# The p7 of the last two first channel products as seven smaller products, with another order of the pair's blocks

## The chip, the cores and the metric

The kernel runs on one core of a Trainium2 chip. The metric is the device time of one execution in microseconds (us); lower is better. Before the change the median of three runs is 796.17 us (796.07, 796.17 and 796.9).

## The reference

The program computes an attention block with a mask from hashes, and an MLP mixer over its output. All inputs are float32. Cut to what is computed:

```python
# q, k, v: (4, 8, 768, 64)
mask = q_bucket[..., :, None] == k_bucket[..., None, :]   # 6 sign bits of q @ proj, k @ proj
scores = np.where(mask, q @ k.T / 8, -1e9)
attn = softmax(scores) @ v            # (B, S, H*D) = x: (4, 768, 512)
h = np.maximum(x.T @ w_tok1, 0) @ w_tok2      # over the 768 tokens
u = x + h.T
h2 = np.maximum(u @ w_ch1, 0) @ w_ch2         # 512 -> 1536 -> 512 channels
out = u + h2
```

The change concerns the first channel product, `u @ w_ch1`, with its ReLU.

## The kernel before, in words

There are three stages, one after the other: attention (one pair of heads at a time), the token mixing, and the channel mixing (`channels`). The 3072 rows of u lie transposed in the on-chip tile `XT` (512 channels in four blocks of 128, by 3072 rows).

`channels` takes the rows in three steps, s = 0, 1, 2, of 1024 rows each (two halves of TT = 512). A step first makes the hidden values (the first channel product with ReLU), then the outputs (`outputs(s)`, the second channel product).

Both products use the Strassen-Winograd scheme: a product of 2 x 2 blocks is made of seven block products p1 to p7 instead of eight, and of sums of the blocks. The left operand is a weight, the right one activations. Sums of weight blocks are in `SW1` and `SW2`, sums of activations in `T[0]` to `T[3]` (buffers `TA` and `TB`). Results go to `R[0]` to `R[3]`.

At s = 0 the hidden values come from `hidden(0, t)` for six t, with whole block products. Between them, jobs of `prepare` make the sums that a second level of the same scheme needs of the weights, and store them, with the raw quarters, to DRAM: `second_parts` for the second channel product, `hidden_parts` for four products of the first (p2, p6, p3, p4). A job makes four sums on the Vector engine (DVE), in one of two scratch places, and issues its stores on SP's queue. One place is the tile `seen`, the other a part of the tile `second1`. The list of jobs has twelve entries, and `hidden` takes one of them in its middle and one after it (call at line 817 and on; jobs at 1057 to 1060, stores at 1068 to 1078).

At s = 1 and 2 the hidden values come from `hidden_pair(s, t, between)` for t = 0, 1, 2 (GP = 3), which makes two of the six blocks at a time. In it p1, p5 and p7 are whole products (`whole`: two groups of matmuls of 512 columns), and p2, p6, p3 and p4 are objects of the class `Smaller`, each of seven matmuls of 256 columns, one second-level product each:

- `one` makes the first quarter product, and the Activation engine (ACT) copies it out of the bank (line 897).
- `three` makes three products that can be added at once to quarters of a bank pair that holds something else already (the "direct quarters").
- `rest` makes the other three; the last of them is added to the bank that ACT copied in `one`. It then issues on SP's queue the fetch of the left parts that stand five objects later (`fetch_hidden_left`, line 860). Left parts of 448 KB lie in five places in turn (`hidden_left_at`).
- `finish` copies a quarter out on ACT (line 918) and makes two sums on DVE (lines 920 and 923).

The right parts of a smaller product are the four quarters of its right block and four sums of them; `right_sums` makes these on DVE (lines 846 to 849) once for each s: p2's in `outputs(s - 1)`, p6's ahead of the first pair, p3's and p4's inside the first pair (`between`).

Four PSUM bank pairs (b0 to b3, two banks of 512 columns each) are given out by hand in `ring`. The engines run in the order that the code is written in (`manual_schedule`), with waits by semaphores where one engine needs another. `plus` (line 955) is an add on DVE, `copy` (952) and `relu` (958) are on ACT. `end_rows` runs the end of the pair before: three ReLUs and the difference r[1] - r[0].

`look()` is another matter: it checks the sizes of q and k, four times a pair. It squares a tile fetched earlier on ACT (lines 1297 and 1298) and has the GpSimd queue (POOL) fetch the next (line 1308). POOL also issues the stores that add to the output (line 1223).

In `outputs(s)`, `product` makes a second-level product of 21 matmul groups, about 9.06 us each, with its right sums made on DVE just ahead (`begin`, lines 1131 and 1132; `combine`, line 1136; lines 1171 and 1174), and `fetch_left` (line 1114) fetches the left parts two products ahead.

All matmuls of `channels` are issued at line 780, in `accumulate`.

Of the kernel before, what the change touches and what calls it, by code (L numbers as in the profile page):

```python
# [36 lines left out]
F32 = mybir.dt.float32  # L37
# [11 lines left out]
def kernel(  # L49
# [13 lines left out]
    nc = tc.nc  # L63
    P = 128
# [9 lines left out]
    NHT = DCH // P  # L74
    HALF = S // 2
    GR = NR // 2
    TT = 512
# [674 lines left out]
    def channels(pool, psum, SW1, second, TA, judge):  # L752
# [7 lines left out]
        last = B * S // (2 * TT) - 1  # L760
# [7 lines left out]
        def bank_pair(i):  # L768
            return psum.tile([P, 2, TT], F32, name=f"b{i}", tag=f"b{i}", bufs=1)
# [66 lines left out]
        def right_sums(name, s):  # L836


            sl = [slice(TT * (2 * s + i), TT * (2 * s + i) + TT) for i in range(2)]
            src = {"p2": XT[:, KC:, sl[0]], "p3": XT[:, KC:, sl[1]], "p6": T[1], "p4": T[3]}[name]  # L840
            z = split4(XT[:, SMALLER.index(name), : 2 * TT])
            half = [slice(0, TT // 2), slice(TT // 2, TT)]
            b = [src[:, k, n] for k in range(2) for n in half]

            def job():
                nc.vector.tensor_tensor(z[:, 0], b[1], b[0], op=ALU.subtract)
                nc.vector.tensor_tensor(z[:, 1], b[3], b[1], op=ALU.subtract)
                nc.vector.tensor_tensor(z[:, 2], b[3], z[:, 0], op=ALU.subtract)
                nc.vector.tensor_tensor(z[:, 3], b[2], z[:, 2], op=ALU.subtract)

            return job, [*b, *(z[:, i] for i in range(4))]

        def split4(a):
            return a.rearrange("p (n t) -> p n t", n=4)

        def fetch_hidden_left(h):

            if h < 4 * GP * last:
                t = h // 4 % GP
                nc.sync.dma_start(  # L860
                    out=hidden_left_at(h).rearrange("p (i c) -> p i c", i=7),
                    in_=hidden_passed[SMALLER[h % 4]][:, :7, P * t : P * t + P],
                )

        def hidden_left_at(h):
# [10 lines left out]
        def first_weight(name):  # L876

            return {
                "p2": WC1[:, KC:, : DCH // 2], "p3": SW1[:, 2], "p4": WC1[:, KC:, DCH // 2 :], "p6": SW1[:, 0],
            }[name]  # L880

        def kept(name):
# [3 lines left out]
        class Smaller:  # L886
# [12 lines left out]
            def three(self, pair, start=False):  # L899

                self.mm(pair[:, 0, : TT // 2], 5, 2, start)
                self.mm(pair[:, 0, TT // 2 :], 3, 3, start)
                self.mm(pair[:, 1, : TT // 2], 6, 7, start)

            def rest(self):
# [19 lines left out]
        def hidden_pair(s, t, between):  # L925


            sl = [slice(TT * (2 * s + i), TT * (2 * s + i) + TT) for i in range(2)]
            ks = range(KC)
            r = [a[:, :, t::GP].rearrange("p n i c -> p i n c") for a in R]  # L930
            x, z, e, y = ring
            ring[:] = [y, e, x, z]

            p1, e2 = [output_at(i).rearrange("p i n -> p (i n)") for i in (0, 2)]
            p5, e6, u = copies(), copies(), copies()
            e3, e4 = p1, e2
            h = 4 * GP * (s - 1) + 4 * t
            p2, p6, p3, p4 = [Smaller(h + i, name, s) for i, name in enumerate(SMALLER)]

            def rows(a):  # L940
                return a.rearrange("p (i n c) -> p i n c", i=2, n=2)

            def banks(a):
                return a.rearrange("p i (n c) -> p i n c", n=2)

            def whole(pair, left, right, which=(0, 1)):
                for i in which:
                    at = P * (t + GP * i)
                    accumulate(pair[:, i], lambda k: left(k)[:, at : at + P], right, ks)

            def copy(to, pair):
                nc.scalar.copy(to.rearrange("p (i n) -> p i n", i=2), pair)

            def plus(to, a, b):
                nc.vector.tensor_tensor(to, a, b, op=ALU.add)

            def relu(i):
                nc.scalar.activation(r[i], r[i], ACT.Relu)

            X = bank_pair(x)  # L960
            whole(X, lambda k: WC1[:, k], lambda k: XT[:, k, sl[0]])
            Z, E = bank_pair(z), bank_pair(e)
            copy(p1, X)
            p2.one(E, e2)
            p2.three(Z, True)
            Y = bank_pair(y)
            whole(Y, lambda k: WC1[:, k, DCH // 2 :], lambda k: T[0][:, k], [0])
            n = TT * 3 // 2
            plus(p1[:, :n], Z.rearrange("p i n -> p (i n)")[:, :n], p1[:, :n])
            end_rows()  # L970
            p2.rest()
            whole(Y, lambda k: WC1[:, k, DCH // 2 :], lambda k: T[0][:, k], [1])
            p2.finish()
            copy(p5, Y)
            look()
            plus(r[0], rows(p1), rows(e2))
            for job in between:
                job()
            E = bank_pair(z)
            p6.one(E, e6)  # L980
            p6.three(X)
            copy(u, X)
            V = bank_pair(e)
            whole(V, lambda k: SW1[:, 1, k], lambda k: T[2][:, k])
            p6.rest()
            look()
            plus(rows(p5), banks(V), rows(p5))
            p6.finish()
            relu(0)
            plus(u, u, e6)  # L990
            E3 = bank_pair(x)
            p3.one(E3, e3)
            look()
            p3.three(Y)
            p4.three(V)
            p4.one(bank_pair(z), e4)
            plus(r[1], banks(Y), rows(u))
            plus(r[2], banks(V), rows(u))
            plus(r[3], rows(p5), rows(u))
            p3.rest()  # L1000
            p4.rest()
            p3.finish()
            plus(r[1], r[1], rows(e3))
            p4.finish()
            plus(r[2], r[2], rows(e4))
            look()

            def end():
                relu(3)
                relu(1)  # L1010
                relu(2)
                nc.vector.tensor_tensor(r[1], r[1], r[0], op=ALU.subtract)

            unfinished.append(end)

        SMALLER = ["p2", "p6", "p3", "p4"]
        GP = HC // 2
        hidden_passed = second["hidden_passed"]  # L1020


# [8 lines left out]
        def prepare():  # L1031
# [42 lines left out]
            def hidden_parts(name):  # L1074
                def store(place, raw, rest):
                    nc.sync.dma_start(out=hidden_passed[name][:, :4], in_=place)
                    for there, here in zip(kept(name), [*raw, rest]):
                        nc.sync.dma_start(out=there, in_=here[:, 0])

                return parts(first_weight(name), store, SMALLER.index(name) % 2 == 0)  # L1080

            sums = weight_sums(WC2, SW2, slice(0, HC), slice(HC, NHT), low, high)
            return [
                [], sums, [whole("p1"), second_parts("p7")], *([second_parts(name)] for name in ("p6", "p3", "p5", "p2", "p4")),
                *([hidden_parts(name)] for name in SMALLER),
            ]

        def area(i):
# [257 lines left out]
        for s in range(1, last + 1):  # L1346
            right_sums("p6", s)[0]()
            for t in range(GP):
                hidden_pair(s, t, [right_sums(name, s)[0] for name in ("p3", "p4")] if t == 0 else [])
                if t == 0:  # L1350
                    residual(s)
            outputs(s)
# [7 lines left out]
    def with_token_weights(stage):  # L1360
        with tc.tile_pool(name="tok", bufs=1, reuse_waits="tile") as tok:
# [7 lines left out]
    n = NHT // 4 * P  # L1369
    second = {  # L1370
        "hidden_passed": {
            f"p{i}": dram.tile([P, 8, NHT // 4 * P], F32, name=f"hidden_left{i}") for i in (2, 3, 4, 6)
        },
        "passed": {
            f"p{i}": dram.tile([P, (4 if i == 1 else 7) * n], F32, name=f"left{i}") for i in range(1, 8)
# [99 lines left out]
```

## Time and profile before

One profiled execution took 795.47 us; its span, from the first instruction of the program to the last, is 793.7 us. The rest of the time is start and end.

| what | value |
|---|---|
| median of the runs | 796.17 us |
| profiled execution | 795.47 us |
| its span | 793.7 us |
| TensorE matmul (PE) busy | 787.1 us, 99% |
| Vector engine (DVE) busy | 660.0 us, 83% |
| Activation engine (ACT) busy | 441.6 us, 56% |
| GpSimd (POOL) busy | 53.5 us, 7% |
| bytes moved by DMA | 138.67 MB, mean 175 GB/s |
| matmul records of 512 columns, line 780, TA and SW (p7, in all three steps) | 72, 592 ns each |
| matmul records of 256 columns, line 780, XT and SW | 96, 379 ns each |

How to read it: a float32 matmul leaves two records, each with its weight load (PEld, 190 ns). The records overlap, so a record's length isn't the time that it takes from the engine; that is the distance from one start to the next. A group line names the line of the code, the engine, the operation, and what it writes and reads (`b<-TA,SW`: into a bank from the tiles TA and SW). A timeline line has the start from the beginning of the span, the length, the engine, line, operation and tiles, how many were merged, and, in brackets, how long the engine was idle before it and who ended that.

Where the stages lie in the span: attention to about 310 us, token mixing to 387.6, `hidden(0, t)` to about 459.6, `outputs(0)` to about 524.3, the three pairs of s = 1 to 591.4, `outputs(1)` to about 656, the three pairs of s = 2 and `outputs(2)` to the end.

### The profile page before, as it was taken

The page shows a single profiled execution, that of the slowest core. Times are in us where ns is not written, and L with a number is a line of the kernel's source. Part 1 is how long each engine was busy: PE and PEld are TensorE (multiplying, and loading weights), DVE is VectorE, ACT ScalarE, POOL GpSimd, SP SyncE. Part 2 cuts the span into 40 slices and gives each one's busy share as a digit, 9 for nine tenths or more (in the row PEclk, how much of TensorE's full clock was granted, in tenths as well). Part 3 has the DMA queues.
Part 4 walks back from the last instruction along what each step waited for, and adds up shares of the span by engine and source line. Part 5 has one row for each costly group of instructions (what it writes and reads, how often), then busy time and mean ns, then how long its engine had stood idle before and what let it go on. Part 6 is the DMA issues. An engine that isn't in the chain of part 4 may idle for free.

```text
span 793.7 us, 12166 instructions
## 1 busy us (share of the span) xinstructions
PE 787.1 (99%) x4661; PEld 464.9 (59%) x4661; DVE 660.0 (83%) x885; ACT 441.6 (56%) x706; POOL 53.5 (7%) x77
## 2 busy tenths in 40 slices
PE   9999999999999999999999999999999999999997
PEld 5444444444444444455544458876667886666886
DVE  5989898988987677999688698988769897778986
ACT  6688888888888886333223221337773335775111
POOL 1000000000000000011121010111110012000001
PEclk9999999999999999999999999999999999999999
DMA  4435353537452415796726993699754578630456
GB/s 164 163 123 163 123 163 123 163 126 239 151 179 85 153 43 168 220 275 175 176 62 228 339 350 140 188 299 294 200 151 143 215 204 195 213 109 1 152 173 158
DMA packets 90974, 138.67 MB, mean 175 GB/s; under 512 B 29656, under 2 KB 63392, under 8 KB 88608
## 3 DMA queue, kind: packets, MB, share of 16 engines
q1 hardware_dynamic: 82752, 112.86, 42.9%
q0 software_dynamic: 7728, 24.64, 14.1%
q8 instruction: 38, 0.62, 0.3%
q10 hardware_dynamic: 432, 0.34, 0.2%
q14 instruction: 24, 0.20, 0.1%
HBM read 97.21 MB, written 33.16 MB: 164 GB/s over the span
## 4 chain that ended last, share of the span: by engine, by line
PE 99%; DVE 0%; issue 0%; DVEq 0%
PE b L780 50%; PE sc L353 20%; PE acc L407 16%; PE t L653 5%; PE t L693 5%; PE sums L431 2%; PE hp L301 1%; PE idle L470 0%; PE hw L325 0%; DVE second L1203 0%; DVE ones L97 0%; PE b L1320 0%; DVEq L1470 0%
## 5 line engine op out<-in xcount | busy, mean ns | idle before, releaser
L360 ACT ACTIVATE e<-sc 128x768 f32<-128x768 f32 x192 | 154.2, 812 | 11.1 <-PE sc L353 10.8
L353 PE MATMUL sc<-qk 64*128 64x384 f32 x768 | 153.1, 484 | 0.0
L780 PE MATMUL b<-R,second 128*128 128x256 f32 (+1 forms) x612 | 150.9, 404 | 0.0
L780 PEld LDWEIGHTS b<-R,second 128*128 128x128 f32 x612 | 116.3, 190 | 31.6 <-issue 17.2
L786 ACT COPY c<-b 128x512 f32<-128x512 f32 (+1 forms) x78 | 37.5, 488 | 169.1 <-PE b L780 159.6
L407 PE MATMUL acc<-e,vn 128*32 128x384 f32 x1536 | 127.0, 486 | 0.0
L392 DVE TENSOR_TENSOR esd<-esd,e 128x768 f32<-128x768 f32 x96 | 92.0, 958 | 10.4 <-ACT e L360 0.5
L407 PEld LDWEIGHTS acc<-e,vn 128*32 128x32 f32 x1536 | 49.9, 110 | 73.9 <-issue 73.3
L353 PEld LDWEIGHTS sc<-qk 64*128 64x128 f32 x768 | 68.4, 188 | 41.8 <-issue 36.7
L780 PE MATMUL b<-XT,WC 128*128 128x256 f32 (+1 forms) x264 | 82.5, 456 | 0.0
L780 PEld LDWEIGHTS b<-XT,WC 128*128 128x128 f32 x264 | 50.2, 190 | 29.6 <-issue 25.1
L353 PE MATMUL sc<-bits 64*128 64x384 bf16 x384 | 62.5, 323 | 0.0
L388 DVE SCALAR_TENSOR_TENSOR esd<-e 128x768 f32<-128x768 f32 x32 | 30.6, 955 | 23.4 <-ACT e L360 23.4
L653 PE MATMUL t<-x,W 128*128 128x512 f32 x96 | 41.8, 593 | 0.0
L353 PEld LDWEIGHTS <-bits 64*128 64x128 bf16 x384 | 18.5, 94 | 33.2 <-issue 8.8
L713 POOL DMA_DIRECT2D XT<-second x8 | 9.9, 1232 | 385.5 <-DVE second L712 368.8
L452 ACT COPY rec<-rec 32x384 f32<-32x384 f32 x64 | 32.6, 510 | 5.0 <-DVE rec L446 4.2
L413 ACT ACTIVATE num<-acc,vsum 128x384 f32<-128x384 f32 x32 | 18.6, 582 | 29.7 <-PE acc L407 29.3
L780 PE MATMUL b<-XT,SW 128*128 128x256 f32 (+1 forms) x120 | 34.6, 422 | 0.0
L780 PE MATMUL b<-TA,WC 128*128 128x512 f32 x72 | 33.8, 592 | 0.0
L780 PE MATMUL b<-TA,SW 128*128 128x512 f32 x72 | 32.9, 592 | 0.0
L395 DVE TENSOR_TENSOR esd<-esd,e 128x768 f32<-128x768 f32 x32 | 30.5, 954 | 1.9
(217 smaller groups left out, 1130.0 us busy)
## 6 DMA issues: line engine op xcount, KB each, us to landing
second<-left SPq DMA_DIRECT2D x18, 1344.0 KB
raw<-in_moe_w_ch SPq DMA_DIRECT2D x16, 768.0 KB
qk<-in_qk SPq DMA_DIRECT2D x15, 768.0 KB
seen<-in_qk POOLq DMA_DIRECT2D x21, 384.0 KB, 4.0
WC<-hidden_left SPq DMA_DIRECT2D x15, 448.0 KB
vn<-in_v SPq DMA_DIRECT2D x16, 384.0 KB
vt<-in_vT SPq DMA_DIRECT2D x16, 384.0 KB
x<-bounced SPq DMA_DIRECT2D x4, 1536.0 KB
```

Of the source, the lines that this page charges most:

```text
L353: nc.tensor.matmul(sc[:, i, :HALF], t[rows, 1, P * c : P * c + P], t[rows, 0, qs], start=start, stop=not start,)
L360: nc.scalar.activation(e, sc[:, :, :HALF], ACT.Exp, scale=SCALE)
L388: nc.vector.scalar_tensor_tensor(self.d, es[0], NR * EPS, es[1], op0=ALU.add, op1=ALU.add,)
L392: nc.vector.tensor_tensor(self.d, self.d, e, op=ALU.add)
L395: nc.vector.tensor_tensor(self.d, self.d, self.es[-1], op=ALU.add)
L407: nc.tensor.matmul(acc[D * i + d : D * i + d + 32], vn[:, i, c, d : d + 32], e[:, i], start=(c == 0), stop=(c == NR - 1),)
L413: nc.scalar.activation(nums[self.n][:, self.half], acc, ACT.Identity, scale=-1.0, bias=vsum,)
L452: nc.scalar.copy(rec[other : other + 32, h], rec[at : at + 32, h])
L653: nc.tensor.matmul(ps, W1[:, r, P * j : P * j + P], x[:, r], start=(r == 0), stop=(r == NR - 1),)
L693: nc.tensor.matmul(ps[at], left, right, start=start, stop=True, skip_group_check=True,)
L780: nc.tensor.matmul(ps, left(k), right(k), start=start and k == ks[0], stop=stop and k == ks[-1], skip_group_check=True,)
L786: nc.scalar.copy(c, ps)
```

## The change

p7 becomes a fifth `Smaller`. What it brings:

- In each of the six pairs, p7's two groups of whole matmuls (four matmuls of 512 columns) become seven matmuls of 256. p7 gets its first quarter `e7` (in the tile `q1`), its `rest` and its `finish`, and one more add, of `e7` to `u`. Its direct quarters fill three quarters of the bank pair V; the fourth stays unused, so the add to p5 takes 768 columns, and r[2] is made in two adds and a copy on ACT.
- p7's right sums are one more job of four DVE operations in the first pair of each s; they lie in `SW1[:, 1]`.
- `hidden_parts("p7")` is one more job at s = 0: four sums and five stores. It shares an entry of the list with p6's, and p7 takes the scratch place in `second1`; p3 moves from that place to `seen`.
- The left parts have five fetches a pair; the object five later is now the same product of the next pair.
- The order inside the pair: p6's direct quarters stand ahead of its first quarter. Behind each first quarter stand the direct quarters of the next product, and then the rest. Behind p4's first quarter stands the first block of the next pair's p1 (`opened`, kept in `ahead`), in the pairs that have a next one. `ring` hands the bank pairs on in another order.
- `Smaller.three` starts the second half of a bank with `start=False`.

```diff
@@ right_sums
-            z = split4(XT[:, SMALLER.index(name), : 2 * TT])
+            if name == "p7":
+                z = SW1[:, 1].rearrange("p k c -> p (k c)")[:, : 2 * TT]
+            else:
+                z = XT[:, ["p2", "p6", "p3", "p4"].index(name), : 2 * TT]
+            z = split4(z)
@@ fetch_hidden_left
-            if h < 4 * GP * last:
-                t = h // 4 % GP
+            if h < 5 * GP * last:
+                t = h // 5 % GP
...
-                    in_=hidden_passed[SMALLER[h % 4]][:, :7, P * t : P * t + P],
+                    in_=hidden_passed[SMALLER[h % 5]][:, :7, P * t : P * t + P],
@@ Smaller.three
-                self.mm(pair[:, 0, TT // 2 :], 3, 3, start)
+                self.mm(pair[:, 0, TT // 2 :], 3, 3, False)
@@ hidden_pair
-            ring[:] = [y, e, x, z]
+            ring[:] = [y, e, z, x]
...
+            e7 = q1.rearrange("p i n -> p (i n)")
-            h = 4 * GP * (s - 1) + 4 * t
-            p2, p6, p3, p4 = [Smaller(h + i, name, s) for i, name in enumerate(SMALLER)]
+            h = 5 * GP * (s - 1) + 5 * t
+            p2, p6, p7, p3, p4 = [Smaller(h + i, name, s) for i, name in enumerate(SMALLER)]
...
-            X = bank_pair(x)
-            whole(X, lambda k: WC1[:, k], lambda k: XT[:, k, sl[0]])
+            def opened(pair, which, s=s, t=t):
+                start = TT * 2 * s
+                whole(pair, lambda k: WC1[:, k], lambda k: XT[:, k, start : start + TT], which, t)
+
+            X = ahead.pop() if ahead else None
+            if not X:
+                X = bank_pair(x)
+                opened(X, [0])
+            opened(X, [1])
...
             copy(p5, Y)
+            plus(r[0], rows(p1), rows(e2))
+            p6.three(X)
+            p6.one(bank_pair(z), e6)
+            copy(u, X)
             look()
-            plus(r[0], rows(p1), rows(e2))
-            for job in between:
+            V = bank_pair(e)
+            for job in between[:2]:
                 job()
-            E = bank_pair(z)
-            p6.one(E, e6)
-            p6.three(X)
-            copy(u, X)
-            V = bank_pair(e)
-            whole(V, lambda k: SW1[:, 1, k], lambda k: T[2][:, k])
+            p7.three(V, True)
             p6.rest()
-            look()
-            plus(rows(p5), banks(V), rows(p5))
+            plus(p5[:, :n], V.rearrange("p i n -> p (i n)")[:, :n], p5[:, :n])
+            for job in between[2:]:
+                job()
             p6.finish()
-            relu(0)
             plus(u, u, e6)
-            E3 = bank_pair(x)
-            p3.one(E3, e3)
+            p7.one(bank_pair(x), e7)
             look()
             p3.three(Y)
+            p7.rest()
+            p7.finish()
+            p3.one(bank_pair(z), e3)
+            relu(0)
             p4.three(V)
-            p4.one(bank_pair(z), e4)
+            p3.rest()
             plus(r[1], banks(Y), rows(u))
-            plus(r[2], banks(V), rows(u))
+            plus(u, u, e7)
+            plus(r[2][:, 0], banks(V)[:, 0], rows(u)[:, 0])
+            plus(r[2][:, 1, 0], banks(V)[:, 1, 0], rows(u)[:, 1, 0])
+            p3.finish()
+            p4.one(bank_pair(x), e4)
+            look()
+            nc.scalar.copy(r[2][:, 1, 1], rows(u)[:, 1, 1])
+            if t + 1 < GP:
+                ahead.append(bank_pair(y))
+                opened(ahead[0], [0], t=t + 1)
+            p4.rest()
             plus(r[3], rows(p5), rows(u))
-            p3.rest()
-            p4.rest()
-            p3.finish()
+            p4.finish()
             plus(r[1], r[1], rows(e3))
-            p4.finish()
             plus(r[2], r[2], rows(e4))
             look()
@@ channels, prepare
-        SMALLER = ["p2", "p6", "p3", "p4"]
+        SMALLER = ["p2", "p6", "p7", "p3", "p4"]
...
-                return parts(first_weight(name), store, SMALLER.index(name) % 2 == 0)
+                return parts(first_weight(name), store, name in ("p2", "p7"))
...
-                *([hidden_parts(name)] for name in SMALLER),
+                [hidden_parts("p2")], [hidden_parts("p6"), hidden_parts("p7")], [hidden_parts("p3")], [hidden_parts("p4")],
@@ the loop over s and t
-                hidden_pair(s, t, [right_sums(name, s)[0] for name in ("p3", "p4")] if t == 0 else [])
+                hidden_pair(s, t, [right_sums(name, s)[0] for name in ("p7", "p3", "p4")] if t == 0 else [])
```

More of the change, by code (lines that the diff above doesn't have):

```diff
@@ L839, in right_sums @@
             sl = [slice(TT * (2 * s + i), TT * (2 * s + i) + TT) for i in range(2)]
-            src = {"p2": XT[:, KC:, sl[0]], "p3": XT[:, KC:, sl[1]], "p6": T[1], "p4": T[3]}[name]
-            z = split4(XT[:, SMALLER.index(name), : 2 * TT])
+            src = {"p2": XT[:, KC:, sl[0]], "p3": XT[:, KC:, sl[1]], "p6": T[1], "p7": T[2], "p4": T[3]}[name]
+            if name == "p7":
[3 more added lines that the diff above has]
+            z = split4(z)
             half = [slice(0, TT // 2), slice(TT // 2, TT)]
@@ L879, in first_weight @@
                 "p2": WC1[:, KC:, : DCH // 2], "p3": SW1[:, 2], "p4": WC1[:, KC:, DCH // 2 :], "p6": SW1[:, 0],
+                "p7": SW1[:, 1],
             }[name]
@@ L944, in banks, with whole @@
                 return a.rearrange("p i (n c) -> p i n c", n=2)
-            def whole(pair, left, right, which=(0, 1)):
+            def whole(pair, left, right, which=(0, 1), t=t):
                 for i in which:
@@ L1014, in hidden_pair @@
             unfinished.append(end)
-        SMALLER = ["p2", "p6", "p3", "p4"]
+        SMALLER = ["p2", "p6", "p7", "p3", "p4"]
         GP = HC // 2
+        ahead = []
         hidden_passed = second["hidden_passed"]
@@ L1371 @@
         "hidden_passed": {
-            f"p{i}": dram.tile([P, 8, NHT // 4 * P], F32, name=f"hidden_left{i}") for i in (2, 3, 4, 6)
+            f"p{i}": dram.tile([P, 8, NHT // 4 * P], F32, name=f"hidden_left{i}") for i in (2, 3, 4, 6, 7)
         },
```

## The prediction

> **What bounds the kernel now.** I read the page's head and chain first, then the chain in order of time, the windows of single stages, and the timelines of the first pair and of SP's queue.
>
> ```profile
> span 793.7 us, 12166 instructions
> ...
> PE 787.1 (99%) x4661; PEld 464.9 (59%) x4661; DVE 660.0 (83%) x885; ACT 441.6 (56%) x706; POOL 53.5 (7%) x77
> ...
> PE 99%; DVE 0%; issue 0%; DVEq 0%
> ```
>
> TensorE is the chain. In order of time (start, length, what) the channel stage is one piece:
>
> ```profile
> 387.63 364.23 PE b L780 x1308
> ...
> 751.97 36.28 PE b L780 x168
> ```
>
> Start-to-start times of the matmuls there are 0.429 us per record of 512 columns and 0.216 per record of 256 (one float32 matmul is two records), with no larger gap. So PE time taken out is worth its full length, and any new wait of PE costs its full length. The windows are the three pairs of s=1, then the stretch in which the parts for later are stored:
>
> ```profile
> 524.27:546.64 22.37, 22.37 (x81) 15.19 (x80) 17.94 (x29) 11.49 (x20) 4.74 (x6) 1.00 1.01 276
> 546.64:569.00 22.36, 22.36 (x81) 15.20 (x80) 16.04 (x19) 16.47 (x27) 2.16 (x4) 1.00 0.81 253
> 569.00:591.40 22.40, 22.40 (x81) 15.21 (x81) 16.08 (x19) 16.47 (x27) 2.15 (x4) 1.00 0.54 151
> ...
> 455.00:470.00 15.00, 15.00 (x37) 6.63 (x36) 13.35 (x21) 3.58 (x7) 3.00 (x4) 1.00 0.96 363
> ```
>
> Columns: length; busy PE, weight load, DVE, ACT, POOL; clock; DMA share; GB/s. A pair takes 22.4 us of PE. DVE has 4.4 us to spare in the first, some 6.3 in the others, ACT 5.9. In 455 to 470 the DMA engines are full.
>
> **What the Trainium skill says.** "TensorE: Matmul & The Clock Gate", section "Wait — 56ns, not 53.3ns?": a warm matmul takes N / 2.4 GHz plus about 2.5 ns. The trace agrees: 1024/2.4 + 2.5 = 429.2 ns, 512/2.4 + 2.5 = 215.8. Smaller blocks cost almost nothing extra. "PSUM — Partial Sum Buffer", section "Engine vs sequencer instructions": ACT and DVE run strictly in order, and matmuls start in order, so what waits holds all behind it; the trace shows no overtaking. "DMA: Bandwidth & Descriptors", section "Queues, rings and completion order": each DMA engine takes a ring's descriptors in order, so an added store delays the loads issued after it on SP. In the trace the load issued at 470.06 follows the stores of 465.05.
>
> **The change, part by part.**
>
> *PE work.* Removed per pair: 4 matmuls of 512 columns, 8 x 0.429 = 3.43 us (535.87 to 539.30 in the first pair). Added: 7 of 256 columns, 14 x 0.216 = 3.02. Gain 0.41 a pair, 2.47 us for six pairs. The next pair's block and the direct quarters only move.
>
> *DVE and ACT per pair.* DVE: + p7's finish (0.69 + 0.42), + adding e7 to u (1.22), - 0.27 for the add to p5 (0.96 for 1.23), - 0.12 for r[2] in two pieces: + 1.9 us, 18 of 22. ACT: three 256-column copies, + 1.1. Both fit; hidden under PE except in the first pair of each s, where DVE also has p7's four sums.
>
> *First pair, layout on the trace's clock.* These rows of before are the anchor:
>
> ```profile
> 531.13 1.46 PE L780 MATMUL b<-XT,WC 128*128 128x256 f32 x6
> 532.63 0.37 ACT L918 COPY second<-b 128x256 f32<-128x256 f32 x1 [3.06 <-PE b L780]
> 533.03 0.69 DVE L920 TENSOR_TENSOR second<-b,second 128x512 f32<-128x512 f32 x1 [2.39 <-ACT second L918]
> 534.14 1.46 PE L780 MATMUL b<-TB,WC 128*128 128x256 f32 x6
> 534.22 1.22 DVE L955 TENSOR_TENSOR R<-second 128x1024 f32<-128x1024 f32 x1
> 536.48 0.42 DVE L849 TENSOR_TENSOR XT<-XT 128x256 f32<-128x256 f32 x1
> 537.95 0.42 DVE L849 TENSOR_TENSOR XT<-TB,XT 128x256 f32<-128x256 f32 x1
> ```
>
> Until 534.14 nothing changes. Then p6 takes four matmuls (1.73) and p7's direct quarters begin at 535.87. Their third needs the last of p7's sums. DVE makes them where it made p3's, so they end at 536.90 (536.48 + 0.42). PE would be there at 536.73. The hand-over to PE: DVE's first memset ends at 1.03 and the weight load waiting for it starts at 1.08, so 0.05; how much of a 0.19 us weight load then lies bare isn't shown for 128 columns, so 0.05 to 0.24; I take 0.14. Stall 0.31. DVE goes on: p3's sums to 538.37, the p5 add to 539.25, p4's sums to 540.7, p6's finish to 541.86. p3's first quarter reuses p6's bank: PE is there at 537.04 + 0.43 + 1.29 + 0.43 + 1.29 + 1.29 = 541.77 and gets it at 542.0: stall 0.23. DVE then has u, p7's finish, r[1], e7, r[2], p3's finish, r[3], p4's finish and the two last adds, 11.6 us, to about 553.5; only then may ACT overwrite e2 (0.04 + 0.37), which p2's rest in the next pair waits for: 554.05, against PE at 542.0 + 11.6 = 553.6 less some 0.2 that DVE's overlapped starts win. Stall 0.2 (0 to 0.6). After that DVE has slack.
>
> *Last pair.* With no next pair, p4's rest stands directly behind p4's first quarter, whose bank ACT must have copied. Matmul start to its end 0.216 + 0.379, to ACT 0.04 (532.59 to 532.63), copy 0.37, hand-over 0.14: 1.15 us, less 0.43 in which the matmul itself runs: stall 0.72 (0.63 to 0.82). In before, p3's rest (1.29) stands there. In the other pairs the opened block, 1.72, covers it; without that cover each would pay 0.72 too.
>
> Sum per s: 0.31 + 0.23 + 0.2 + 0.72 = 1.46, twice 2.9 (2.2 to 4.0).
>
> *Storing p7's parts at s=0.* Four DVE sums (2.2) fall in DVE's gap of 3.76 us before 456.40; the first waits for the store of p2's, whose buffer it takes, about 454.5, so they end at 456.7: DVE 0.3 late, nothing lost. Five stores, 1536 KB = 1.57 MB, at 363 GB/s: 4.3 us more in a full queue.
>
> ```profile
> 452.67 0.32 SPq L1076 DMA_DIRECT2D hidden_left<-seen  x1
> 453.03 3.69 SPq L1078 DMA_DIRECT2D hidden_left<-SW  x4
> 459.70 0.32 SPq L1076 DMA_DIRECT2D hidden_left<-second  x1
> ...
> 464.69 0.32 SPq L1076 DMA_DIRECT2D hidden_left<-seen  x1
> 465.05 2.86 SPq L1078 DMA_DIRECT2D hidden_left<-WC  x4
> 470.06 0.32 SPq L1114 DMA_DIRECT2D second<-left  x1
> ```
>
> p3 now uses `seen`, and p4 right after it, so p4's sums on DVE wait until p3's store has landed: about 462.6 + 4.3 less overlap = 466.4 instead of 462.45, and all DVE work of `outputs(0)` stands 4 us back behind it. These show what it has in hand:
>
> ```profile
> 462.45 0.55 DVE L1057 TENSOR_TENSOR seen<-WC 128x384 f32<-128x384 f32 x1
> ...
> 471.36 0.96 DVE L1171 TENSOR_TENSOR R<-R 128x768 f32<-128x768 f32 x1 [1.37 <-PE b L780]
> 472.66 0.96 DVE L1174 TENSOR_TENSOR R<-R 128x768 f32<-128x768 f32 x1 [0.34 <-PE b L780]
> ```
>
> L1171 would end at 474.9 and PE wants it at 475.05: just in time. 2.3 us of delay are left for the next `begin` (b01 ready at 481.9, wanted by 481.36: 0 to 0.5). p4's stores go out at 468.7 instead of 464.69, so the load of the second product's left parts (L1114, in before landed at 478.2 by its semaphore's last update, wanted at 478.9) lands at 478.7 to 480.7. Both waits overlap. I take 0.5, bounds 0 and 2.2.
>
> *Fetches of left parts in the pairs*: one more per pair (448 KB), each with a pair's length, some 19 us, from issue to use; in before they land 4 to 7 us after issue. Nothing. POOL's order of looks and stores is kept; nothing.
>
> **Sum.** Profiled execution 795.47 (span 793.7): - 2.47 + 2.9 + 0.5 = + 0.9, so 796.4. The three runs' median, 796.17, lies 0.7 above it: 797.1. Bounds: - 2.47 + 2.2 + 0 = - 0.3 (795.9) and - 2.47 + 4.0 + 2.2 = + 3.7 (799.9). About 0.2%, 1.6 us, is what a measurement of this kernel can tell from no change. So: within it, slightly slower.
>
> **Rivals.**
> - *The store backlog decides (slower).* In the stage change at 460 to 480, DVE or PE waits for SP's queue. For it: DMA share 0.96, the load's 0.7 us in hand, the new back-to-back use of `seen`. Against: DVE's idle 1.7 us and the pauses in the queue. From 1.2 us of stall there the whole is slower; at 2.2 it is 796.17 - 2.47 + 2.9 + 2.2 = 798.8.
> - *ACT or DVE falls behind in every pair (slower).* ACT would do 17.6 of 22 us with looks between the critical copies; one us per pair of late copies gives 797.1 + 6 = 803. Against: between first quarter and rest stand 1.29 us, for a round trip of 1.15.
> - *The waits vanish (faster).* If DVE starts the first pair earlier and hand-over is 0.05, only the last pair's 0.63 remains: 796.17 - 2.47 + 1.3 = 795.0; with less still 794.3.
>
> **How the numbers follow.** Forecast case (795.6 to 797.8) 0.54; backlog 0.25, of which nearly all is slower; late copies 0.11; vanished waits 0.10, most of it faster by over 0.2%. That is faster 0.08, same 0.55, slower 0.37. The range 795.4 to 800.4 takes in the forecast's bounds and the backlog, and leaves out the late copies and half of the last.
>
> **What would show it.** PE busy down by about 2.5 us while the span grows; 14 records more per pair of 256 columns and 8 fewer of 512; gaps on PE before the third direct quarter of p7 in the first pair of each s (0.3), before p3's first quarter (0.2), and before p4's rest in the last (0.7); one DVE wait of some 4 us at `seen` near 462. Wrong: a gap over 1 us before the second product's first matmul near 479, gaps in the middle pairs, or none in the last.

## The result and the profile after

The changed kernel takes 797.86 us (median of 15 runs, 797.23 to 798.45), the kernel before 796.17 (15 runs, 794.3 to 797.73). The ratio is 1.0021, with a 95% interval of 1.0013 to 1.0029: 1.7 us slower. The sign is that of the forecast (797.1); the size lies 0.8 us beyond its number, at the edge of the 0.2% that I had called no difference.

The head of the page, and TensorE's share of the chain that ended last:

```profile
span 796.7 us, 12316 instructions
...
PE 786.7 (99%) x4697; PEld 471.0 (59%) x4697; DVE 675.4 (85%) x921; ACT 448.0 (56%) x724; POOL 53.8 (7%) x77
...
PE 92%; DVE 4%; DMA 3%; issue 0%; ACT 0%; DVEq 0%
```

The span grew by 3.0 us, and PE is no longer the whole chain: DVE and DMA hold 7% of it. The line says where to look, not how much is lost. A DVE step stands in the chain with its whole length although PE was busy during most of it; the loss is only what PE itself stands still. PE busy fell by 0.4 us and not by the 2.5 that the prediction named as a sign: it takes in small waits, and it differs between profiles with the same matmuls (787.1 in before, 786.4 in reuse_only). Followed in order of time, the chain leaves PE at 443.83 and comes back at 482.57 (start, length, what):

```profile
447.23 7.11 DMA hidden_left<-second
...
461.84 5.08 DMA hidden_left<-seen
...
466.94 0.56 DVE seen L1080
...
474.49 0.88 DVE R L1194
...
482.57 51.16 PE b L780 x224
```

That is the storing of the parts at s=0. The windows answer to the four of before; columns as there:

```profile
523.90:546.80 22.90, 22.83 (x89) 16.51 (x88) 19.69 (x35) 11.48 (x22) 4.21 (x5) 1.00 0.99 263
546.80:569.20 22.40, 22.40 (x88) 16.36 (x87) 18.39 (x23) 17.83 (x32) 2.16 (x4) 1.00 0.93 301
569.20:592.00 22.80, 22.34 (x89) 16.53 (x88) 18.47 (x24) 18.32 (x33) 2.17 (x4) 1.00 0.60 177
455.00:470.00 15.00, 15.00 (x37) 6.81 (x37) 11.41 (x20) 3.52 (x7) 1.81 (x2) 1.00 0.92 358
```

Busy PE hides small gaps, since the page models where a matmul ends. So I took the distance from start to start of neighbouring matmuls and subtracted the 0.216 or 0.429 us that their width costs. What is over I call a gap. In before one distance of the channel stage is more than 0.01 us over, by 0.11 at 751.80 in the last `outputs`; every run has it, and the prediction's "no larger gap" missed it. In after the following come on top. The next matmul record is always 0.07 to 0.10 late as well, because its weight load had nothing to hide behind (behind the gap at 475.50 this load ends at 475.77 and the record starts at 475.79); the last column has both:

| where | waits for | us |
|---|---|---|
| 472.0, outputs(0), first product | VectorE | 0.10 |
| 475.50, same | VectorE, L1194 | 0.88 |
| 482.57, second product, third of its seven parts | VectorE, L1155 | 0.59 |
| first pair, before p7's third direct quarter, each s | VectorE, p7's last sum | 0.33 |
| first pair, before p3's first quarter, each s | VectorE, p6's finish | 0.17 |
| second pair, before p2's rest, each s | ScalarE, e2's copy | 0.12 |
| last pair, before p4's rest, each s | ScalarE, e4's copy | 0.73 |
| 781.51, last product | load of its left parts | 1.24 |

Storing 1.58, pairs 1.36 twice, the last one 1.24: 5.54 us. From the start of the first to the start of the last channel matmul (L780) after takes 403.46 us, before 400.39, so 3.07 more; 5.54 less the 2.47 of matmul time saved is 3.07. Nothing is missing. This stage length repeats to 0.01 us where no wait differs, much better than the time of a run, and I use it below.

The profile names who ends these waits:

```profile
PE b L780 <- DMA second<-left: 1.0, 1, 1.0
PE b L780 <- ACT second L902: 0.9, 2, 0.5
PE b L780 <- ACT c L786: 0.6, 1, 0.6
PE b L780 <- DVE R L1155: 0.4, 1, 0.4
```

(Releaser, total us, times, longest.) ACT's L786 in the third line is a false name for the gap at 475.50. In a second profile of the same kernel that gap stands under `DVE R L1194`, and there, as in one variant (last_covered), PE starts before the ACT copy beside it has ended; in all seven profiles with the gap PE starts 0.15 us after VectorE's sum. The list also leaves out gaps of 0.3 and less.

The pairs, as forecast (timeline; p7's last sum and the matmul behind it, then the copy and the matmul of the last pair):

```profile
537.61 0.42 DVE L853 TENSOR_TENSOR SW<-TA,SW 128x256 f32<-128x256 f32 x1
538.08 0.30 PEld L780 LDWEIGHTS b<-SW,WC 128*128 128x128 f32 x2 [0.47 <-DVE SW L853]
538.09 0.70 PE L780 MATMUL b<-SW,WC 128*128 128x256 f32 x2
...
590.84 0.37 ACT L902 COPY second<-b 128x256 f32<-128x256 f32 x1
591.26 1.56 PE L780 MATMUL b<-XT,SW 128*128 128x256 f32 x6 [0.46 <-ACT second L902]
```

And SP's queue with VectorE beside it at s=0:

```profile
457.61 0.32 SPq L1099 DMA_DIRECT2D hidden_left<-second  x1
457.98 3.77 SPq L1101 DMA_DIRECT2D hidden_left<-SW  x4
461.84 0.53 SPq L1099 DMA_DIRECT2D hidden_left<-seen  x1
462.41 3.42 SPq L1101 DMA_DIRECT2D hidden_left<-SW  x4
469.18 0.32 SPq L1099 DMA_DIRECT2D hidden_left<-seen  x1
```

```profile
462.94 0.69 DVE L834 TENSOR_TENSOR R<-R,R 128x512 f32<-128x512 f32 x1
466.94 0.56 DVE L1080 TENSOR_TENSOR seen<-WC 128x384 f32<-128x384 f32 x1 [3.31 <-DMA hidden_left<-seen]
...
474.40 0.95 DVE L1194 TENSOR_TENSOR R<-R 128x768 f32<-128x768 f32 x1
```

p3's store (461.84) goes out right behind p7's five, and VectorE stands 3.3 us until it has landed, because p4's sums take the same buffer (the prediction's sign was a wait of some 4 us). Here L1194 and L1155 are the lines that before has as L1171 and L1132.

### The profile page after: what moved, and what is told of

Read it like the earlier page. It is cut to its first block, busy times and chain, and to the rows that moved or that the text cites. A ratio compares the mean times of both kernels' runs of the same rounds, so it can differ in the third digit from the quotient of the medians.

```text
span 796.7 us, 12316 instructions
## 1 busy us (share of the span) xinstructions
PE 786.7 (99%) x4697; PEld 471.0 (59%) x4697; DVE 675.4 (85%) x921; ACT 448.0 (56%) x724; POOL 53.8 (7%) x77
## 4 chain that ended last, share of the span: by engine, by line
PE 92%; DVE 4%; DMA 3%; issue 0%; ACT 0%; DVEq 0%
PE b L780 43%; PE sc L353 20%; PE acc L407 16%; PE t L653 5%; PE t L693 5%; PE sums L431 2%; DMA second<-left 1%; PE hp L301 1%; DMA hidden_left<-second 1%; DMA hidden_left<-seen 1%; DVE R L1159 0%; PE idle L470 0%; DVE R L961 0%; PE hw L325 0%; DVE second L1082 0%
## 5 line engine op out<-in xcount | busy, mean ns | idle before, releaser
L780 PE MATMUL b<-R,second 128*128 128x256 f32 (+1 forms) x612 | 151.6, 405 | 2.0 <-DMA second<-left 1.0
L780 PEld LDWEIGHTS b<-R,second 128*128 128x128 f32 x612 | 115.9, 190 | 34.8 <-issue 17.2
L786 ACT COPY c<-b 128x512 f32<-128x512 f32 (+1 forms) x78 | 37.5, 488 | 173.5 <-PE b L780 162.1
L780 PE MATMUL b<-XT,WC 128*128 128x256 f32 (+1 forms) x228 | 75.4, 470 | 0.0
L780 PEld LDWEIGHTS b<-XT,WC 128*128 128x128 f32 x228 | 43.1, 190 | 27.5 <-issue 21.0
L780 PE MATMUL b<-XT,SW 128*128 128x256 f32 (+1 forms) x156 | 44.0, 414 | 0.9 <-ACT second L902 0.9
L780 PE MATMUL b<-TA,WC 128*128 128x512 f32 (+1 forms) x108 | 43.6, 521 | 0.0
L780 PEld LDWEIGHTS b<-XT,SW 128*128 128x128 f32 x156 | 29.3, 190 | 13.0 <-issue 6.0
## 6 DMA issues: line engine op xcount, KB each, us to landing
WC<-hidden_left SPq DMA_DIRECT2D x18, 448.0 KB
```

Of the source, the lines that this page charges most:

```text
L780: nc.tensor.matmul(ps, left(k), right(k), start=start and k == ks[0], stop=stop and k == ks[-1], skip_group_check=True,)
L786: nc.scalar.copy(c, ps)
```

## The experiments

Theory: the change saves 2.47 us of TensorE time and pays it back in these waits; each has its own cause and can be taken away alone. Rivals: VectorE or ScalarE lacks room in general, so that a wait taken away comes back elsewhere; the load at 781 belongs to the change; and, for the storing, bytes against buffers. Ratios are to runs of the kernel before on the same chip. The last column is the stage length less before's 400.39.

| kernel | median us | ratio (95%) | stage, us against before |
|---|---|---|---|
| after | 797.86 | 1.0021 (1.0013 to 1.0029) | +3.07 |
| after_again | 797.55 | 1.0023 (1.0014 to 1.0032) | +1.66 |
| store_only | 797.60 | 1.0021 (1.0011 to 1.0031) | +1.52 |
| bytes_only | 795.95 | 0.9998 (0.9989 to 1.0006) | 0.00 |
| reuse_only | 796.28 | 1.0003 (0.9995 to 1.0011) | 0.00 |
| bytes_reuse | 797.89 | 1.0029 (1.0017 to 1.0041) | +1.45 |
| p7_early | 795.95 | 1.0003 (0.9995 to 1.0012) | +0.26 |
| last_covered | 796.73 | 1.0009 (1.0002 to 1.0016) | +0.71 |
| sums_early | 796.13 | 1.0004 (0.9996 to 1.0013) | +1.82 |
| no_ahead | 800.11 | 1.0057 (1.0041 to 1.0072) | +4.66 |
| all_three | 792.88 | 0.9963 (0.9951 to 0.9976) | -2.47 |

### The storing alone: store_only

```
+                "p7": SW1[:, 1],
...
-                return parts(first_weight(name), store, SMALLER.index(name) % 2 == 0)
+                return parts(first_weight(name), store, name in ("p2", "p7"))
...
-                *([hidden_parts(name)] for name in SMALLER),
+                [hidden_parts("p2")], [hidden_parts("p6"), hidden_parts("p7")], [hidden_parts("p3")], [hidden_parts("p4")],
```

The DRAM tensor that p7's parts go to is added as well, here and in bytes_only and bytes_reuse.

> The kernel before, with p7's parts summed and stored at s=0 as the change does it (same slot, same two places); nothing reads them, so this adds unused stores to the computation and alters nothing else. Theory (the storing of p7's parts costs 1.58 us of TensorE waits, by way of VectorE, at the start of the first outputs): slower than before by 1.2 to 1.9 us, with TensorE gaps of some 0.9 us near 475 and 0.6 us near 482 and no new gap elsewhere. Rival (what was measured comes from the pairs and from the load of left parts near 781; the storing costs the 0.5 us of the prediction): slower by 0.3 to 0.7 us.

Ratio 1.0021, and three gaps, at 471.87, 475.05 and 482.12, of 0.04, 0.88 and 0.59 us; none elsewhere. The storing alone makes the kernel as much slower as the whole change does, since what the pairs save and what they wait for (2.47 against 2.72 us) nearly cancel. The rival's 0.3 to 0.7 fell.

### The storing moved: p7_early

```
-                return parts(first_weight(name), store, name in ("p2", "p7"))
+                return parts(first_weight(name), store, name in ("p2", "p3"))
...
-                [], sums, [whole("p1"), second_parts("p7")], ...
-                [hidden_parts("p2")], [hidden_parts("p6"), hidden_parts("p7")], [hidden_parts("p3")], [hidden_parts("p4")],
+                [hidden_parts("p7")], sums, [whole("p1"), second_parts("p7")], ...
+                *([hidden_parts(name)] for name in ("p2", "p6", "p3", "p4")),
```

> The changed kernel, with p7's parts summed and stored in the first, empty slot of the list instead of the one of p6, so that p2, p6, p3 and p4 are stored as in the kernel before. Theory: the two gaps near 475 and 482 go and nothing comes in their place, so 1.4 to 1.6 us faster than the changed kernel, about 796.3. Rival (the gaps come from the length of SP's queue as a whole, not from the buffer used twice in a row): under 0.4 us faster. If the wait of 1.24 us for left parts near 781 belongs to the change, it is in this profile too; if it was chance of one execution, it is not.

795.95 us, ratio 1.0003 against 1.0021 for after, 1.4 us less. All gaps of `outputs(0)` are gone; the pairs' eight stay, 2.72 us, and 2.72 - 2.47 = 0.25 is the +0.26 of the stage. The same bytes stored earlier cost nothing. The edit takes away both the longer queue ahead of p3's store and the buffer used twice in a row, so it doesn't tell the two apart; the next runs do.

### Bytes against buffers: bytes_only, reuse_only, bytes_reuse

bytes_only, on the kernel before:

```
+            def hidden_raw():
+                (a00, a01), (a10, a11) = weight_quarters(SW1[:, 1])
+                for i, here in enumerate([a00, a01, a11, a10] * 2):
+                    nc.sync.dma_start(out=hidden_passed["p7"][:, i], in_=here[:, 0])
-                *([hidden_parts(name)] for name in SMALLER),
+                [hidden_parts("p2")], [hidden_parts("p6"), hidden_raw], [hidden_parts("p3")], [hidden_parts("p4")],
```

> The kernel before, with 1536 KB more stored at s=0 in the slot of p6: eight stores of p7's raw quarters, which nothing reads, with no sums on VectorE and no buffer of the parts used more often than before. So it adds unused stores to the computation and alters nothing else. Theory (the storing costs time because VectorE waits for the buffers of the parts, not because the queue is longer): no TensorE gap near 475 or 482, at most the load of the second product's left parts late near 479 by 0 to 0.8 us; 0 to 0.8 us slower than before. Rival (the bytes in the queue cost it): a gap of over 1 us near 479 and 1.2 to 2.2 us slower than before.

reuse_only, on the kernel before; bytes_reuse has both edits:

```
-                return parts(first_weight(name), store, SMALLER.index(name) % 2 == 0)
+                return parts(first_weight(name), store, name == "p2")
```

> The kernel before with nothing but p3's parts made in the buffer that p4's take right after; no store is added. Theory (reuse costs only where the queue is longer): p3's store, issued near 459.7, is in by about 463, so VectorE waits 0.2 to 1 us at p4's sums, TensorE not at all; within 0.2 us of the kernel before. Rival (reuse alone makes the wait): gaps of over 0.5 us near 475 and 482, 0.5 to 1.6 us slower.

> The kernel before with the same 1536 KB of unused stores as in bytes_only, and with p3's parts made in the buffer that p4's take right after (as in the changed kernel), instead of the one that p2's left; p7's sums still not made. Theory (bytes and reuse together are the cost: VectorE then waits for p3's store ahead of p4's sums and the sum behind them, 3.1 us of work that in bytes_only was done before the wait, which ended at 468.06): VectorE's first sum of p4 starts near 468, TensorE gaps of 1.4 to 1.7 us near 475 and 0.4 to 1.0 near 482, and 1.8 to 2.6 us slower than before. Rival (what made VectorE late are p7's own sums, 2.2 us and 1.0 more where GpSimd's add stood beside one): gaps of 0.5 us at most, and under 0.6 us slower.

Neither edit alone costs anything: no gap, stage +0.00 both times. Together they cost 1.45 us, nearly the 1.52 of store_only, without p7's sums being made at all. So the cost of the storing is the joint one of a longer queue and a buffer used twice in a row; the rival that VectorE's work on p7's sums makes it late fell, since the loss comes without them. (In reuse_only and bytes_reuse p6's parts, p3's and p4's all take `seen`, so p3's sums are late for another reason, the wait for p6's store. On before's clock, that is, shifted by how much earlier the stage begins, they start at 458.54 in bytes_reuse and at 459.02, behind p7's sums, in after.) My number for bytes_reuse, 1.8 to 2.6, was above the stage's 1.45, though the ratio, 2.3 us with an interval from 1.4 to 3.3, allows it: I put VectorE's first sum of p4 near 468, and it came at 466.77. VectorE's rows show how the two act together. bytes_only:

```profile
463.94 0.56 DVE L1060 TENSOR_TENSOR seen<-WC,seen 128x384 f32<-128x384 f32 x1
464.42 0.95 DVE L1141 TENSOR_TENSOR TA<-R,R 128x768 f32<-128x768 f32 x1
468.06 0.96 DVE L1136 TENSOR_TENSOR second<-R 128x768 f32<-128x768 f32 x1 [2.69 <-DMA hidden_left<-second]
...
472.53 0.95 DVE L1176 TENSOR_TENSOR R<-R 128x768 f32<-128x768 f32 x1
```

reuse_only:

```profile
463.61 0.56 DVE L1057 TENSOR_TENSOR seen<-WC 128x384 f32<-128x384 f32 x1 [0.45 <-DMA hidden_left<-seen]
...
471.07 0.95 DVE L1171 TENSOR_TENSOR R<-R 128x768 f32<-128x768 f32 x1
```

bytes_reuse:

```profile
458.03 0.56 DVE L1057 TENSOR_TENSOR seen<-SW 128x384 f32<-128x384 f32 x1 [0.98 <-DMA hidden_left<-seen]
...
466.77 0.56 DVE L1057 TENSOR_TENSOR seen<-WC 128x384 f32<-128x384 f32 x1 [3.67 <-DMA hidden_left<-seen]
...
474.23 0.95 DVE L1176 TENSOR_TENSOR R<-R 128x768 f32<-128x768 f32 x1
```

bytes_only has a wait of 2.69 us too, and it ends later, at 468.06. It is harmless because p4's sums and the first sum of `outputs(0)` (463.94 and 464.42 are their last two rows), 3.1 us of work, were done ahead of it; in bytes_reuse they stand behind it. The sum that TensorE needs (L1176) starts at 472.53 in the one and at 474.23 in the other, and only the second is too late. A wait's length says less than what is queued behind it.

### The last pair's cover: last_covered

```
             p4.three(V)
-            p3.rest()
+            if t + 1 < GP:
+                p3.rest()
...
-            p3.finish()
+            if t + 1 < GP:
+                p3.finish()
             p4.one(bank_pair(x), e4)
+            if t + 1 == GP:
+                p3.rest()
+                p3.finish()
```

> The changed kernel, with p3's rest and finish behind p4's first quarter in the last pair of each s, so that ScalarE's copy of that quarter is covered, as in the kernel before. Theory: the gap of 0.73 us before p4's rest goes in both s; p3's rest and p4's first quarter themselves find nothing late: 1.2 to 1.5 us faster than the changed kernel. Rival (p7's finish on VectorE is then too late for the bank that p4's first quarter takes, 1.72 us after p7's rest instead of 3.0): a new gap of 0.3 to 0.7 us before p4's first quarter takes the place, and the gain is 0 to 0.7 us.

Both were right in part, and the gain lies between their ranges. The 0.73 before p4's rest is gone in both s, and a smaller gap stands ahead of p4's first quarter, where p7's finish has not yet left the bank:

```profile
588.46 0.42 DVE L928 TENSOR_TENSOR q<-b,q 128x256 f32<-128x256 f32 x1
...
589.03 0.67 PE L780 MATMUL b<-TB,SW 128*128 128x256 f32 x2
```

Its distance is 0.17 us too long, and the next 0.07: 0.25 lost of 0.73 gained, twice. That makes 0.96, and the ratio went from 1.0021 to 1.0009 (0.0012 of 796 us is 0.96).

### p7's sums ahead of the pairs: sums_early

```
             right_sums("p6", s)[0]()
+            right_sums("p7", s)[0]()
...
-                hidden_pair(s, t, [right_sums(name, s)[0] for name in ("p7", "p3", "p4")] if t == 0 else [])
+                hidden_pair(s, t, [right_sums(name, s)[0] for name in ("p3", "p4")] if t == 0 else [])
...
-            for job in between[:2]:
+            for job in between[:1]:
...
-            for job in between[2:]:
+            for job in between[1:]:
```

> The changed kernel, with p7's four sums of the right side made together with p6's ahead of the first pair of each s, instead of between p6's direct quarters and p7's. Theory: the gaps of 0.33, 0.17 and 0.12 us in the first pair and at the start of the next go, 0.4 to 0.6 us per s, 0.8 to 1.2 us in all. Rival (VectorE, which has 4 us to spare in the first pair, is late there by the same 1.7 us at another place): the gaps move ahead of the first pair, to its first rest or to the first product, and the time stays within 0.3 us of the changed kernel.

All three gaps of the first and second pair are gone in both s, 1.25 us, just over the 0.8 to 1.2 expected, and none came in their place; the ratio fell by 0.0017, 1.35 us. The profiled execution has a wait for left parts at 781.04, 1.16 us. It is one of two among 13 that took 797.9 and 798.0; the other eleven lie between 795.55 and 796.48.

### The opened block: no_ahead

```
-            if t + 1 < GP:
-                ahead.append(bank_pair(y))
-                opened(ahead[0], [0], t=t + 1)
```

> The changed kernel without the next pair's opened block: every pair begins with both of its own blocks, and p4's rest stands directly behind p4's first quarter in all three pairs. Theory (the block covers ScalarE's copy of the first quarter, as the price of 0.72 us per uncovered copy says): four more gaps of 0.73 us, less the two of 0.12 at the second pair's start, so 2.6 to 2.9 us slower than the changed kernel. Rival (the copy's wait is not additive: what TensorE loses there it gets back from later waits on VectorE in the same pair): under 1.5 us slower.

2.6 us slower than after_again, measured on the same chip. Every pair now has the wait, with the same distance (0.73 us with the weight load behind it) six times:

```profile
PE b L780 <- ACT second L902: 2.8, 6, 0.5
```

The second pair's 0.12 is gone, as expected, and no other gap of the pairs changed by more than 0.01 us. So as cover the block is worth 0.73 us in each of the four pairs that have one behind them, less the two times 0.12.

### A second profile: after_again

> The changed kernel once more, unaltered, for a second profile. Theory (the wait of 1.24 us for left parts near 781 is chance of single executions, since two of the three variants of the changed kernel whose profiles could show it have it not): the other gaps come again within 0.1 us each, about 1.58 us near 475 and 482 and 1.36 us in each s; the one near 781 may be there or not. Rival (it belongs to the change): it is there, at 1.0 to 1.3 us.

The gaps come again (1.42 us at 475 to 483, 1.33 and 1.35 in the pairs), the one near 781 does not; stage +1.66. Of seven profiles of the changed kernel and its variants it is in two, both of executions among the slowest of theirs. So it goes with single executions. None of the five profiles of before and its variants has it; whether the change makes it more frequent isn't shown. The load in question was issued at 771.50 in after; of the 16 updates of its semaphore 15 had come by 779.01 and the last came at 781.47. "DMA: Bandwidth & Descriptors", section "Why a DMA increments its semaphore by 16 and not by 1", says that the engines of a DMA finish independently and only the full 16 means that all has landed; the trace shows what one late engine costs. What kept that engine wasn't tried and stays open.

### All mended: all_three

p7_early and sums_early together, and in the last pair one matmul of p3's rest ahead of p4's first quarter and two behind it:

```
             p4.three(V)
-            p3.rest()
+            p3.rest1()
+            if t + 1 < GP:
+                p3.rest2()
...
             p4.one(bank_pair(x), e4)
+            if t + 1 == GP:
+                p3.rest2()
+                p3.finish()
```

> The changed kernel with p7's parts stored in the first slot, p7's right sums made ahead of the first pair, and, in the last pair of each s, p3's rest cut in two: one matmul of it ahead of p4's first quarter (0.43 us, for the 0.25 that was missing in the run where all of it came behind), two behind it (0.86 us, for a copy that needs 0.72). Theory (the change's gain of 2.47 us was paid back in these named waits, and nothing else): no TensorE gap is left from 387 us on but perhaps the chance one near 781, and the time is 2.0 to 2.5 us below the kernel before, about 793.5 if that is at 795.8. Rival (VectorE or ScalarE has no room for p7's work, so that a mended wait comes back at the next place): under 1.5 us below the kernel before, with gaps of over 0.3 us at new places.

792.88 us, ratio 0.9963 (0.9951 to 0.9976): 2.9 us (1.9 to 3.9) below the kernel before, and 0.6% below the changed one. The 2.0 to 2.5 expected lies in this interval. Page and chain:

```profile
span 790.5 us, 12316 instructions
...
PE 784.1 (99%) x4697; PEld 471.8 (60%) x4697; DVE 676.2 (86%) x921; ACT 448.0 (57%) x724; POOL 52.3 (7%) x77
...
PE 99%; DVE 0%; issue 0%; DVEq 0%
```

```profile
387.03 361.76 PE b L780 x1344
```

No distance is too long but the 0.11 us that every run has. The stage is 397.92 us, 2.47 below before, to the hundredth what the matmul count says. VectorE and ScalarE do the same work as in after (676.2 and 448.0 us against 675.4 and 448.0), so neither lacked room: the rival fell.

## Why the prediction was right in direction and short in size

Point by point:

- *PE work, 2.47 us saved.* Exact: the stage of all_three. (The formula for a matmul's time fits with N as twice the columns, 1024 for 512 float32 columns, which the prediction used without saying so.)
- *First pair, 0.31 and 0.23; next pair's p2 rest, 0.2.* Measured 0.33, 0.17, 0.12. The layout by hand on the trace's clock was good to 0.1 us. Cause shown by sums_early.
- *Last pair, 0.72.* Measured 0.73; cause shown by last_covered, and by no_ahead with the price in six places. That the opened block covers it in the other pairs is shown. Sum of the pairs 2.72 for 2.9 predicted.
- *Storing p7's parts, 0.5 with bounds 0 and 2.2.* Measured 1.58 in after, 1.42 in its second profile, 1.52 alone. The mechanism named is the right one (p3's parts and p4's in one buffer behind a longer queue, as bytes_reuse shows), and so is the order of the sums behind it; the mis-sized term is the time at which p3's store lands. I wrote "about 462.6 + 4.3 less overlap = 466.4". On before's clock (the stage starts 0.46 later there) VectorE's sum started at 467.40, a full 1.0 us later. By the last update of its semaphore p3's store landed at 463.21 in before and, on the same clock, at 467.38 in after, 4.2 us later.

  So the 4.3 for the bytes was nearly right; the base was 0.6 too early, and the 0.5 taken off for overlap wasn't there. From 452 to 468 the DMA engines of after are busy to 0.95 or more in every microsecond, so p7's bytes put p3's store off by nearly their whole time. reuse_only shows the reuse without the bytes: p3's own sums first wait 0.92 us for p6's store in the same buffer, a wait I hadn't listed, and p4's start at 463.99 on before's clock. There the DMA engines stand almost idle from 460 to 461 (share 0.12), and the bytes fill this pause: they add 3.3 us to it (bytes_reuse, 467.28). In after p3's sums don't wait, since p7's keep VectorE past the landing of p6's store (458.16).

  The step "L1171 would end at 474.9 and PE wants it at 475.05: just in time" had 0.15 us in hand, but PE starts only 0.15 after such a sum's end. The sum ended at 475.81 on before's clock, 0.9 late, which became the stall of 0.88; the second wait (0 to 0.5 predicted) was 0.59. One more reading was off without a cost: p7's sums ended at 458.05 on before's clock, not at 456.7; 1.0 of the difference is one sum that took 1.57 us (last section).
- *The load of the second product's left parts, landing at 478.7 to 480.7, overlapping the other wait.* In bytes_reuse PE waits for it at 479.70, in last_covered at 479.83; in after it doesn't show. In both the later wait, for the next `begin` on VectorE, is shorter by about as much: 0.48 for the load and 0.11 for `begin` in bytes_reuse, 0.50 and 0.10 in last_covered, against 0.59 for `begin` alone in after. In no_ahead the load alone costs 0.61, at 480.02, and `begin` nothing. (The profile names VectorE's L1156 there, but the load's last semaphore update, at 479.89, comes 0.14 us ahead of PE's start, as in the other two.) They do overlap.
- *Fetches of left parts in the pairs, nothing.* No wait for them in any profile of the pairs.
- *Late copies in every pair (803) and vanished waits (795.0).* Neither; the middle pairs have no gap but the 0.12.

Without the chance wait the terms are - 2.47 + 2.72 + 1.58 = + 1.83; the medians differ by 1.69. With 0.5 for the storing the sum would have been + 0.75, inside what I called indistinguishable. The one term that failed carried the result across that line. I had given "the store backlog decides" 0.25 with 1.2 us as the point from which it does; 1.58 is past that point, so this rival is what happened, at less than its full price of 2.2. The time came out inside the range because the bounds for the storing reached to 2.2; the 0.5 that I took was a third of the cost.

## What to carry to other kernels

Where one engine is the whole chain, add up work saved and every wait made, one by one; here a few small waits of different causes ate up a real gain of 2.47 us, and each went away by moving a step, not by doing less. Before putting a store into a full queue, list every buffer whose next use waits for a store behind it, and count what stands behind that wait on its engine: bytes alone and reuse alone cost nothing, together 1.45 us. A margin of 0.15 us at the end of a chain of estimated landings should be priced as a likely stall.

## What the runs showed of the hardware that was not expected

VectorE's sum with both inputs in SBUF takes 0.56 us for 384 columns, and 1.5 to 1.7 in each of the six profiles in which p7's sums stand at 455 us, beside GpSimd's add. From after, VectorE and then GpSimd:

```profile
454.84 0.55 DVE L1081 TENSOR_TENSOR second<-SW 128x384 f32<-128x384 f32 x1
455.42 1.57 DVE L1082 TENSOR_TENSOR second<-second,SW 128x384 f32<-128x384 f32 x1
```

```profile
455.31 1.27 POOL L821 TENSOR_TENSOR c<-c 128x512 f32<-128x512 f32 x1 [10.74 <-ACT c L786]
```

The sum ends 0.4 us after GpSimd's add, a little less than a sum's own 0.56. "SBUF — State Buffer", section "SBUF: two separate sides", says that such a VectorE operation and a GpSimd operation that reads SBUF exclude each other for the whole instruction; the rows agree. I hadn't priced it, though before's trace has two such sums beside that add (1.51 us at 420.08 and 1.57 at 431.85). By the trace it cost nothing here: p7's store, issued behind these sums at 457.61, still stood behind p6's in the queue, the last of which landed at 460.17. No run took this wait away alone.

A matmul that has waited is followed by one that is late too: a 128x128 weight load without cover adds 0.07 us in some places and 0.10 in others. I had put 0.14 for hand-over and load together; the pairs' sizes came out right with it.
